# Later conversion of three weight quarters, and v pooled by additions, in a fused attention and two-MoE kernel

## The chip, the cores and the metric

The kernel runs on one core of a Trainium2 chip. The metric is the device time of one launch in microseconds, the median of several runs. A profile of one further execution shows what every engine did: TensorE (PE, matmuls; its weight loads are PEld), VectorE (DVE), ScalarE (ACT), GpSimd (POOL), and SyncE (SP), whose queue issues all the transfers of this kernel.

## The reference

Three layers follow each other. 8 sequences of 576 tokens give 4608 tokens, the model has 512 columns and 8 heads of 64.

```python
def _attn_ref(q, k, v):
    ...
    k_p = k.reshape(B, H, Sp, pool, D).mean(axis=3)      # 576 rows -> 72
    v_p = v.reshape(B, H, Sp, pool, D).mean(axis=3)
    scores = scale * np.matmul(q, k_p.transpose(0, 1, 3, 2))
    ...                                                  # softmax
    return np.matmul(attn, v_p).astype(np.float32)

def _moe_ref(x, w_in, w_out):
    h = x @ w_in                                         # 512 -> 2048
    r = np.maximum(h, 0.0)
    g = r * r
    return (g @ w_out).astype(np.float32)                # 2048 -> 512

def _moe2_ref(x, phi, w1, w2):                           # soft MoE: 8 experts, 32 slots
    logits = x @ phi
    ...
    return (c @ slot_out).astype(np.float32)
```

The weights `w_in` and `w_out` arrive as 64-bit floats.

## The kernel before, in words

The 4608 tokens are 36 tiles of 128. For each tile the attention's result x (4 blocks of 128 columns) goes into the first layer. That layer is the bulk of the work: for a tile t and a quarter j of w_in's 2048 columns, a **unit** (t, j), it does 12 matmuls of 128x512 (L453) into one PSUM buffer named `l1`, in two halves of 6. There are two such buffers. ACT takes a relu of the result (L466, into `r`), and DVE (L473) or ACT (L475) multiplies, which gives `g`. A third unit can only start when the `g` (where DVE made it, it reads the PSUM buffer itself) of the first is done. Each `g` is stored to DRAM (L477).

The order of everything else is a table: `at(slot, fn)` hangs a step behind the half unit with that number, 288 slots in all. `paced` holds a step until the last relu before it, `pinned(name, ...)` until a marked instruction, `behind_l1` until the last matmul of the first layer. The scheduler then sets each engine's order, and every engine works through its own queue in order: an instruction that waits holds all that stand behind it.

Two kinds of side work lie in the first 250 us, and the change touches both.

**Weights.** A quarter of a 64-bit weight matrix is loaded as four pieces of 512 KB (`load_w`, L373) into one of two staging buffers, `st0` and `st1`, which take turns over the eight loads (four of w_in, four of w_out). Each piece is one chunk and is turned into 32-bit numbers by six instructions (`f32_steps`): ACT L342, then DVE L344, L347 and L351, then an addition L355 and the last DVE step L356. For w_out all of the last five are on DVE, and the result overwrites the staging buffer. Chunk c of w_out's quarter j stands at slot s0 + 3c with s0 = 26 + 12j. At s0 + 13 the quarter is stored (L413), at s0 + 14 to s0 + 17 PE transposes it (L418) and ACT copies it out (L420, `wt`), at s0 + 22 a product with phi follows (L426, copied by DVE L428 to `at_sb`), at s0 + 25 another (L434).

**Pooling.** k and v of one sequence come in four pieces of two heads (72 rows x 1024 numbers, L150) into a ring of three `kv` buffers. Groups of 8 tokens are added up. For sequences 0, 1 and 2 (`PEP`) PE does it for k, and `pool_v_dve` for v: one DVE reduction (L189) that reads the 1024 numbers with a stride. For sequence 3 and later, `pool_kv` does three additions on POOL for each piece, of 512, 256 and 128 columns (L157, L158, L159).

Of the kernel before, what the change touches and what calls it, by code (L numbers as in the profile page):

```python
# [11 lines left out]
U32 = mybir.dt.uint32  # L12
# [5 lines left out]
def kernel(  # L18
# [12 lines left out]
    nc = tc.nc  # L31
# [8 lines left out]
    P = 128  # L40
# [22 lines left out]
    stp = ctx.enter_context(tc.tile_pool(name="stp", bufs=1))  # L63
# [10 lines left out]
    vpp = (kvp, a3)  # L74
# [24 lines left out]
    q_t, raw_k, raw_v, kp_t, vp_t = {}, {}, {}, {}, {}  # L99
# [259 lines left out]
        )  # L359
        yield dst  # L360

    st_t, mark, n_st = {}, {}, [0]
    eng = {"P": nc.gpsimd, "V": nc.vector}
    w_in64 = w_in.bitcast(U32).rearrange("(k p) (f two) -> p k f two", p=P, two=2)
    w_out64 = w_out.bitcast(U32).rearrange("(c p) (d two) -> p c d two", p=P, two=2)

    def load_w(kind, j, i0=0, i1=4):
        if i0 == 0:
            st_t[kind, j] = stp.tile([P, 4, 512, 2], U32, tag=f"st{n_st[0] % 2}", name="st")
            n_st[0] += 1  # L370
        src = w_in64[:, :, j * QF:(j + 1) * QF] if kind == "in" else w_out64[:, j * CPQ:(j + 1) * CPQ]
        for i in range(i0, i1):
            nc.sync.dma_start(out=st_t[kind, j][:, i], in_=src[:, i])  # L373
# [393 lines left out]
    def at(slot, fn, *a):  # L767
        ev.setdefault(slot, []).append((fn, a))
# [64 lines left out]
    for t in range(6, NT):  # L833
# [3 lines left out]
    units = [  # L837
        (0, 0), (0, 1), (1, 0), (3, 1), (3, 0), (1, 1), (2, 0), (0, 2),
        (2, 1), (2, 2), (1, 2), (3, 2), (0, 3), (2, 3), (3, 3), (1, 3),
    ]  # L840
    units += [(t + u, j) for t in range(NI, NT, 2) for j in range(NQ) for u in range(2)]

    for j in range(PC, NQ):
        for kk in range(KD):
            at(CS[j - 2][kk], paced, conv_in, j, kk)
    at(0, load_w, "in", 2)
    at(3, load_w, "in", 3)
    for j in range(NQ):
        s0 = 26 + 12 * j
        at((17, 31, s0 - 8, s0 - 8)[j], load_w, "out", j)  # L850
        for c in range(CPQ):
            at(s0 + 3 * c, paced, conv_out, j, c)
        at(s0 + 13, store_wo, j)
        for kk in range(KD):
            at(s0 + 14 + kk, behind_l1, turn_wo, j, kk)
        at(s0 + 22, behind_l1, fold_phi, j)
        at(s0 + 25, behind_l1, sum_a, j)
# [11 lines left out]
    for t in (NT - 4, NT - 2):  # L869
        s0 = SLOTS * t  # L870
# [13 lines left out]
    for t in range(0, ND, 2):  # L884
        s0 = 96 + 28 * (t // 2)
# [5 lines left out]
    for b in range(1, B):  # L891
        s0 = a_at[b * S // P]
        for i in range(NPAIR):
            at(s0 - 16 + 2 * i, load_kv, k, raw_k, b, i)
            if b in PEP:
                at(s0 - 12 + 2 * i, pool_k, b, i)
            else:
                at(s0 - 12 + 2 * i, pool_kv, nc.gpsimd, raw_k, kp_t, b, i, kvp, "kp")
            at(s0 - 10 + 2 * i, load_kv, v, raw_v, b, i)
            if b in PEP:  # L900
                at(s0 - 4 + 2 * b - 2 + 2 * i, pool_v_dve, b, i, vpp[b % 2])
            else:
                at(s0 - 4 + 2 * i, pool_kv, nc.gpsimd, raw_v, vp_t, b, i, vpp[b % 2], "vp")
        if b not in PEP:
            at(s0 - 4, make_kb, b)
# [271 lines left out]
```

## Time and profile before

| | |
|---|---|
| median of 3 runs | 774.43 us (772.29 to 775.55) |
| the profiled execution | 766.02 us |
| its span, first to last instruction | 764.2 us |
| PE busy | 723.5 us (95%) |
| DVE busy | 532.0 us (70%) |
| ACT busy | 392.1 us (51%) |
| POOL busy | 132.1 us (17%) |
| mean granted clock of TensorE | 0.980 of full speed |

The profiled execution was 8.4 us shorter than the median of the runs. An engine's busy time is the sum over its instructions; the share is that of the span. Whether an engine's wait matters is not seen from the share but from the chain of waits: who released whom, and what PE stood idle for.

### The profile page before, as it was taken

Reading aid. Unit: us, or ns where it says so; the run is one execution under the profiler, and the core shown is the slowest. Engines: PE = TensorE matmul, PEld = TensorE weight load, DVE = VectorE, ACT = ScalarE, POOL = GpSimd, SP = SyncE. Lnnn points to the kernel's source line nnn. Section 1 sums busy time; section 2 is a strip of 40 time slices with the busy share of each in tenths; the row PEclk is TensorE's granted clock in tenths of the full one; section 3 lists DMA queues with packets and bytes.
Section 4 is the critical chain, followed back from the end, with each engine's and each line's share of the span. In section 5 each row is a group of like instructions: output and inputs, shape, how many; then the busy total and the mean of one; then the engine's idle time right before and its main releaser. Section 6 shows DMA issues by size and latency. Waiting matters only on the chain.

```text
span 764.2 us, 14453 instructions
## 1 busy us (share of the span) xinstructions
PE 723.5 (95%) x5260; PEld 511.4 (67%) x5260; DVE 532.0 (70%) x1049; ACT 392.1 (51%) x1135; POOL 132.1 (17%) x151
## 2 busy tenths in 40 slices
PE   8789999989899999999999999999999999998992
PEld 7557788777677776676666666766666676663462
DVE  4996766596936689789979787878787746324153
ACT  3685677455547464545656562737575454341142
POOL 2231300052714400050342221320000000000000
PEclk9699999999999999999999999999999999999997
DMA  8956754858655996696997788878686436979998
GB/s 276 310 181 204 232 134 135 247 146 250 166 166 151 281 250 183 185 275 177 256 285 224 194 243 241 227 216 240 177 271 199 116 96 233 415 250 352 372 313 294
DMA packets 224135, 175.10 MB, mean 229 GB/s; under 512 B 75072, under 2 KB 186688, under 8 KB 224064
## 3 DMA queue, kind: packets, MB, share of 16 engines
q1 hardware_dynamic: 224064, 174.17, 75.2%
q8 instruction: 42, 0.69, 0.4%
q14 instruction: 29, 0.24, 0.1%
HBM read 126.94 MB, written 47.19 MB: 228 GB/s over the span
## 4 chain that ended last, share of the span: by engine, by line
PE 71%; DVE 12%; DMA 7%; ACT 6%; issue 2%; SPq 0%; POOL 0%; ACTq 0%; DVEq 0%
PE l L453 44%; PE misc L633 3%; PE pl L541 3%; PE misc L1098 2%; PE gT L311 2%; ACT es L245 2%; PE att L311 2%; PE l L1066 2%; PE gT L234 2%; PE att L234 2%; PE att L541 2%; DMA kv<-in_v_dram 1%; ACT aT L284 1%; DMA st<-in_moe_w_in_dram 1%; DMA out_dram<-o 1%
## 5 line engine op out<-in xcount | busy, mean ns | idle before, releaser
L453 PE MATMUL l<-w,xh 128*128 128x512 f32 x1152 | 383.4, 412 | 10.1 <-DVE g L473 5.0
L453 PEld LDWEIGHTS l<-w,xh 128*128 128x128 f32 x1152 | 209.8, 190 | 77.1 <-issue 17.1
L453 PE MATMUL l<-w,xl 128*128 128x512 f32 x576 | 231.7, 403 | 0.0
L466 ACT ACTIVATE r<-l 128x512 f32<-128x512 f32 x144 | 86.6, 604 | 163.6 <-PE l L453 151.1
L453 PEld LDWEIGHTS l<-w,xl 128*128 128x128 f32 x576 | 109.3, 190 | 28.7 <-issue 3.9
L157 POOL TENSOR_TENSOR kv<-kv 72x512 f32<-72x512 f32 x40 | 54.0, 1356 | 211.6 <-DMA kv<-in_v_dram 112.8
L284 ACT COPY aT<-turned 32x256 f32<-32x256 f32 (+1 forms) x168 | 67.8, 404 | 21.2 <-DVE turned L293 19.2
L473 DVE TENSOR_TENSOR g<-l,r 128x512 f32<-128x512 f32 x57 | 39.0, 683 | 28.0 <-ACT r L466 21.8
L245 ACT ACTIVATE es<-att,mx 128x72 f32<-128x72 f32 x120 | 36.9, 334 | 25.3 <-DVE mx L241 25.0
L516 DVE STREAM_TRANSPOSE turned<-turned 128x1024 f32<-128x1024 f32 x39 | 47.6, 1230 | 2.5 <-DMA turned<-g_dram 1.9
L245 ACT ACTIVATE es<-gT,mx 128x72 f32<-128x72 f32 x120 | 36.8, 331 | 16.0 <-DVE mx L241 15.9
L286 DVE COPY aT<-turned 32x256 f32<-32x256 f32 (+1 forms) x120 | 38.4, 320 | 1.6
L475 ACT ACTIVATE g<-r 128x512 f32<-128x512 f32 x54 | 34.5, 640 | 0.8
L396 POOL TENSOR_TENSOR w<-tmp,w 128x512 fp32r<-128x512 f32 x16 | 22.8, 1430 | 66.6 <-ACT w L395 66.6
L158 POOL TENSOR_TENSOR kv<-kv 72x256 f32<-72x256 f32 x40 | 33.1, 833 | 0.8
L473 DVE TENSOR_TENSOR tmp<-l,r 128x512 f32<-128x512 f32 x33 | 22.5, 682 | 15.4 <-ACT r L466 12.1
L268 DVE TENSOR_TENSOR es<-es,rs 128x576 f32<-128x576 f32 x36 | 32.3, 902 | 0.7
L344 DVE TENSOR_SCALAR tmp<-tmp 128x512 uint32<-128x512 uint32 x32 | 16.3, 511 | 23.3 <-ACT tmp L342 23.3
L516 DVE STREAM_TRANSPOSE tmp<-tmp 128x1024 f32<-128x1024 f32 x25 | 30.3, 1223 | 2.9 <-DMA tmp<-g_dram 2.9
L342 ACT ACTIVATE tmp<-st 128x512 f32<-128x512 f32 x32 | 21.7, 680 | 14.5 <-DMA st<-in_moe_w_in_dram 10.3
L245 ACT ACTIVATION_READ_ACCUMULATOR es<-att,mx 128x1 f32 x120 | 26.3, 219 | 0.0
L245 ACT ACTIVATION_READ_ACCUMULATOR es<-gT,mx 128x1 f32 x120 | 26.0, 217 | 0.0
(200 smaller groups left out, 1064.1 us busy)
## 6 DMA issues: line engine op xcount, KB each, us to landing
g_dram<-g SPq DMA_DIRECT2D x95, 256.0 KB
turned<-g_dram SPq DMA_DIRECT2D x39, 512.0 KB
w<-in_moe_w_dram SPq DMA_DIRECT2D x32, 512.0 KB
tmp<-g_dram SPq DMA_DIRECT2D x25, 512.0 KB
w<-in_moe_w_dram SPq DMA_DIRECT2D x6, 2048.0 KB
g_back<-g_dram SPq DMA_DIRECT2D x40, 256.0 KB
kv<-in_k_dram SPq DMA_DIRECT2D x32, 288.0 KB
kv<-in_v_dram SPq DMA_DIRECT2D x32, 288.0 KB
```

Source lines behind the costliest of these rows:

```text
L157: eng.tensor_tensor(out=x[:, :, 0:4], in0=x[:, :, 0:4], in1=x[:, :, 4:8], op=ALU.add)
L158: eng.tensor_tensor(out=x[:, :, 0:2], in0=x[:, :, 0:2], in1=x[:, :, 2:4], op=ALU.add)
L245: mark["es", t] = nc.scalar.activation(out=es[:, e], in_=sv[:, h], func=AF.Exp, bias=mx[:, e:e + 1], accum_out=rsum[:, t % 8, e, 0:1],)
L268: mark["norm", t] = nc.vector.tensor_tensor(out=es, in0=es, in1=rs.unsqueeze(2).to_broadcast([P, H, SP]), op=ALU.mult)
L284: nc.scalar.copy(out=dst, in_=src)
L286: eng[e].tensor_copy(dst, src)
L453: mm = mark["l1", t, j] = nc.tensor.matmul(hp_t[t, j], steps[i][0], steps[i][1], start=(i == 0), stop=(i == 2 * n - 1))
L466: nc.scalar.activation(out=r, in_=hp, func=AF.Relu, scale=1.0 / (R * R if sq == "V" else R))
L473: mark["sq"] = nc.vector.tensor_tensor(out=dst, in0=pre, in1=src, op=ALU.mult)
L475: nc.scalar.activation(out=dst, in_=src, func=AF.Square)
L516: nc.vector.transpose(out=gc.rearrange("p (n i) -> p n i", i=32), in_=gc.rearrange("p (n f) -> p n f", f=32))
L541: mark["logits"] = nc.tensor.matmul(pl[32 * c:32 * c + 32], a_sb[:, c, 32 * j:32 * j + 32], gT[:, c], start=(alone or j == 0), stop=(alone ...
```

## The change

For the last three quarters of w_out the whole group of steps moves to later slots: s0 goes from 26, 38, 50, 62 to 26, 40, 54, 70, so by 0, 2, 4 and 8 half units. The loads go from slots 17, 31, 42, 54 to 20, 28, 45, 59. The staging buffer no longer alternates by a counter: quarter j of w_in uses `st0` for even j, quarter j of w_out uses `st1` for even j. w_out's quarter 0 so follows w_in's quarter 3 and its quarter 1 follows w_in's quarter 2, which is free sooner. For v of the sequences 1 and 2, the reduction L189 is replaced by the three additions of `pool_kv`, on DVE; those of sequence 2 are held until the latest `g` that DVE makes, those of sequence 1 until a matmul of the first unit.

```diff
-    st_t, mark, n_st = {}, {}, [0]
+    st_t, mark = {}, {}
...
         if i0 == 0:
-            st_t[kind, j] = stp.tile([P, 4, 512, 2], U32, tag=f"st{n_st[0] % 2}", name="st")
-            n_st[0] += 1
+            st_t[kind, j] = stp.tile([P, 4, 512, 2], U32, tag=f"st{(j + (kind == 'out')) % 2}", name="st")
...
     for j in range(NQ):
-        s0 = 26 + 12 * j
-        at((17, 31, s0 - 8, s0 - 8)[j], load_w, "out", j)
+        s0 = (26, 40, 54, 70)[j]
+        at((20, 28, 45, 59)[j], load_w, "out", j)
...
             if b in PEP:
-                at(s0 - 4 + 2 * b - 2 + 2 * i, pool_v_dve, b, i, vpp[b % 2])
+                at(
+                    s0 - 4 + 2 * b - 2 + 2 * i, pinned, ("l1", units[0][0], 0) if b == 1 else "sq",
+                    pool_kv, nc.vector, raw_v, vp_t, b, i, vpp[b % 2], "vp",
+                )
             else:
                 at(s0 - 4 + 2 * i, pool_kv, nc.gpsimd, raw_v, vp_t, b, i, vpp[b % 2], "vp")
```

The lines L342 to L477 of the kernel before stand one line earlier in the changed one from L373 on (L473 is L472 there).

The first place is DVE around the `g` of unit (6, 0), the first unit of tile 6, where v of sequence 2 is pooled. `vp_1635` (`vp_1643` in the changed kernel) is the pooled v, `st_1133` and `st_1076` are the staging buffer of w_out's quarter 1, `l1_1587` and `l1_1589` the result of unit (6, 0). The kernel before, in DVE's order:

```order
L189 TENSOR_REDUCE vp_1635<-kv_1495 72x128
L351 SCALAR_TENSOR_TENSOR tmp_124<-st_1133,tmp_124 128x512
L189 TENSOR_REDUCE vp_1635<-kv_1540 72x128
L428 COPY at_sb_1599<-misc_1594 128x4x4x32
L355 TENSOR_TENSOR tmp_124<-tmp_124 128x512
L189 TENSOR_REDUCE vp_1635<-kv_1585 72x128
L473 TENSOR_TENSOR g_1613<-l1_1587,r_1614 128x512
```

The changed kernel at the same `g`:

```order
L171 TENSOR_SCALAR kb0_119<-att_1544 64x72
L427 COPY at_sb_1601<-misc_1596 128x4x4x32
L472 TENSOR_TENSOR g_1615<-l1_1589,r_1616 128x512
L157 TENSOR_TENSOR kv_1424<-kv_1424 72x2x256
L344 TENSOR_SCALAR tmp_124<-tmp_124 128x512
L347 TENSOR_SCALAR tmp_124<-tmp_124 128x512
L158 TENSOR_TENSOR kv_1424<-kv_1424 72x2x128
L351 SCALAR_TENSOR_TENSOR tmp_124<-st_1076,tmp_124 128x512
L159 TENSOR_TENSOR vp_1643<-kv_1424 72x128
L472 TENSOR_TENSOR g_1681<-l1_1647,r_1682 128x512
```

All pooling of sequence 2's v moved from ahead of this `g` to behind it; its first piece now stands, with part of a conversion, ahead of the next `g` of DVE, that of unit (7, 0).

The second place is DVE at the conversions of w_out's quarter 2 (`st_1783`) in the kernel before, around the `g` of units (8, 0) and (9, 0):

```order
L473 TENSOR_TENSOR g_1971<-l1_1951,r_1972 128x512
L344 TENSOR_SCALAR tmp_124<-tmp_124 128x512
L347 TENSOR_SCALAR tmp_124<-tmp_124 128x512
L351 SCALAR_TENSOR_TENSOR tmp_124<-st_1783,tmp_124 128x512
...
L241 TENSOR_REDUCE mx_1989<-gT_1998 128x4
L344 TENSOR_SCALAR tmp_124<-tmp_124 128x512
L347 TENSOR_SCALAR tmp_124<-tmp_124 128x512
L351 SCALAR_TENSOR_TENSOR tmp_124<-st_1783,tmp_124 128x512
L473 TENSOR_TENSOR g_2063<-l1_2006,r_2064 128x512
```

In the changed kernel DVE comes from the `g` of unit (8, 0) to that of (9, 0), `g_2045`, and of (8, 1), `g_2103`, with attention's steps alone, and then meets two conversions of quarter 3 (`st_1893`) ahead of the `g` of unit (8, 2), `g_2204`:

```order
L472 TENSOR_TENSOR g_2045<-l1_1995,r_2046 128x512
...
L472 TENSOR_TENSOR g_2103<-l1_2053,r_2104 128x512
L344 TENSOR_SCALAR tmp_124<-tmp_124 128x512
L347 TENSOR_SCALAR tmp_124<-tmp_124 128x512
L351 SCALAR_TENSOR_TENSOR tmp_124<-st_1893,tmp_124 128x512
L355 TENSOR_TENSOR tmp_124<-tmp_124 128x512
L356 SCALAR_TENSOR_TENSOR st_1893<-tmp_124 128x512
L344 TENSOR_SCALAR tmp_124<-tmp_124 128x512
L347 TENSOR_SCALAR tmp_124<-tmp_124 128x512
L351 SCALAR_TENSOR_TENSOR tmp_124<-st_1893,tmp_124 128x512
L472 TENSOR_TENSOR g_2204<-l1_2191,r_2205 128x512
```

No conversion stands between the `g` of (8, 0) and of (9, 0) any more; two stand ahead of that of (8, 2), three units after (9, 0).

The third place is SP's queue, where the first two loads of w_out are issued. Before, `st_858` is quarter 0 and `st_1133` quarter 1:

```order
L373 DMA st_858<-in_moe_w_out_dram 128x1024 x4
...
L150 DMA kv_1255<-in_k_dram 72x2x512
L150 DMA kv_1310<-in_k_dram 72x2x512
L150 DMA kv_1382<-in_k_dram 72x2x512
L477 DMA g_dram2_104<-g_898 128x4x128
L373 DMA st_1133<-in_moe_w_out_dram 128x1024 x4
```

After, `st_1076` is quarter 1 and `st_905` quarter 0:

```order
L372 DMA st_1076<-in_moe_w_out_dram 128x1024 x4
...
L150 DMA kv_1263<-in_k_dram 72x2x512
L372 DMA st_905<-in_moe_w_out_dram 128x1024 x2
L476 DMA g_dram2_104<-g_893 128x4x128
L372 DMA st_905<-in_moe_w_out_dram 128x1024 x2
L150 DMA kv_1318<-in_k_dram 72x2x512
L476 DMA g_dram2_104<-g_938 128x4x128
L150 DMA kv_1384<-in_k_dram 72x2x512
```

The two loads changed places: the quarter that is converted first is now loaded second, at the place where quarter 1 stood, and ahead of two loads of k instead of behind them.

## Rows read from the trace of the kernel before

**Rows 1.** The page: busy time of the engines, and the chain that ended last.

```profile
PE 723.5 (95%) x5260; PEld 511.4 (67%) x5260; DVE 532.0 (70%) x1049; ACT 392.1 (51%) x1135; POOL 132.1 (17%) x151
...
PE 71%; DVE 12%; DMA 7%; ACT 6%; issue 2%; SPq 0%; POOL 0%; ACTq 0%; DVEq 0%
```

**Rows 2.** What PE waited for, 126 to 232 us: total, times, longest.

```profile
PE l L453 <- DVE g L473: 4.3, 2, 2.7
PE gT L299 <- ACT wt L420: 1.0, 1, 1.0
```

**Rows 3.** PE's timeline: start, duration, [idle before <- releaser].

```profile
196.06 0.60 PE L418 MATMUL gT<-ident,st 128*128 128x128 f32 x4
199.34 0.73 PE L453 MATMUL l<-w,xh 128*128 128x512 f32 x2 [2.67 <-DVE g L473]
...
210.76 0.66 PE L311 MATMUL gT<-aT,vp 72*64 72x128 f32 x8
```

**Rows 4.** L453 in three stretches: length, PE busy, PEld busy, granted clock, DMA.

```profile
147.29:150.09 2.80, 2.80 (x14) 2.24 (x12) 1.00 0.70 217
156.30:159.29 2.99, 2.99 (x9) 2.34 (x7) 0.50 1.07 374
200.99:203.13 2.14, 2.14 (x7) 1.65 (x5) 0.50 0.91 158
```

**Rows 5.** 20 us of all engines: PE, PEld, DVE, ACT, POOL busy, clock, DMA.

```profile
140.00:160.00 20.00, 18.40 (x124) 14.18 (x121) 14.50 (x22) 7.87 (x27) 6.48 (x5) 0.91 0.80 261
```

**Rows 6.** DVE's timeline around the `g` of unit (6, 0).

```profile
146.83 2.01 DVE L189 TENSOR_REDUCE vp<-kv 72x128 f32<-72x1024 f32 x1 [2.03 <-DMA kv<-in_v_dram]
...
152.46 1.91 DVE L189 TENSOR_REDUCE vp<-kv 72x128 f32<-72x1024 f32 x1
154.28 0.69 DVE L473 TENSOR_TENSOR g<-l,r 128x512 f32<-128x512 f32 x1
```

**Rows 7.** The chain that ended last, in order of time: two transfers of v.

```profile
133.77 3.88 DMA kv<-in_v_dram
139.67 7.13 DMA kv<-in_v_dram
```

**Rows 8.** DVE's timeline ahead of the third stall.

```profile
190.17 1.50 DVE L347 TENSOR_SCALAR tmp<-tmp 128x512 uint32<-128x512 uint32 x1
191.71 1.10 DVE L351 SCALAR_TENSOR_TENSOR tmp<-st,tmp 128x512 f32<-128x512 uint32 x1
...
198.60 0.69 DVE L473 TENSOR_TENSOR g<-l,r 128x512 f32<-128x512 f32 x1
```

**Rows 9.** ACT's timeline there: the relu of the same unit.

```profile
195.60 0.63 ACT L466 ACTIVATE r<-l 128x512 f32<-128x512 f32 x1
```

**Rows 10.** POOL's timeline: first additions of sequence 3.

```profile
152.24 1.42 POOL L157 TENSOR_TENSOR kv<-kv 72x512 f32<-72x512 f32 x1 [59.25 <-PE gT L234]
...
188.67 2.71 POOL L157 TENSOR_TENSOR kv<-kv 72x512 f32<-72x512 f32 x2 [7.54 <-DMA kv<-in_k_dram]
```

**Rows 11.** DVE operations by line: count, ns min/median/max, first and last start.

```profile
L347 DVE TENSOR_SCALAR tmp<-tmp x32: 409/420/1504, 11.0 to 206.2; 128x512 uint32<-128x512 uint32 x32
L351 DVE SCALAR_TENSOR_TENSOR tmp<-st,tmp x32: 674/692/1646, 11.5 to 207.2; 128x512 f32<-128x512 uint32 x32
L189 DVE TENSOR_REDUCE vp<-kv x10: 1905/1980/2030, 17.3 to 152.5; 72x128 f32<-72x1024 f32 x10
L355 DVE TENSOR_TENSOR tmp<-tmp x32: 670/688/1342, 12.2 to 208.0; 128x512 f32<-128x512 f32 x32
L556 DVE TENSOR_TENSOR plsb<-plsb,att x21: 277/603/648, 286.3 to 682.8; 128x256 f32<-128x256 f32 x15, 128x128 f32<-128x128 f32 x6
```

**Rows 12.** SP's timeline: the second load of w_out.

```profile
88.14 1.80 SPq L373 DMA_DIRECT2D st<-in_moe_w_out_dram  x4
```

**Rows 13.** ACT's timeline: the first chunk of w_out, and the relu after it.

```profile
94.65 0.71 ACT L342 ACTIVATE tmp<-st 128x512 f32<-128x512 f32 x1
...
96.63 0.60 ACT L466 ACTIVATE r<-l 128x512 f32<-128x512 f32 x1 [0.75 <-PE l L453]
```

## The prediction

> **What bounds the kernel now.** I read the busy times first: PE works 95% of the span and owns 71% of the chain that ended last, DVE 12% [rows 1]. So the kernel is a PE stream with a few holes. A step on another engine counts only where PE stands still for it, and since PE is the bound to the end, a hole that is closed in the middle shortens the whole. The second view is what PE waited for, in the stretch where conversion of w_out and pooling of v meet, 126 to 232 us. It names three holes, two on a `g` made by DVE, 4.3 us together, and one of 1.0 us on ACT's copy of a transposed w_out [rows 2]. The larger of the two is 2.67 us at 199.34 [rows 3], so the other is 1.6 us and the sum of all three 5.3 us.
>
> The third view is the granted clock around them. Twelve matmuls L453 took 2.80 us at clock 1.00 (0.233 us each), but seven took 2.99 us behind the first hole and five took 2.14 us behind the third, both at 0.50 [rows 4]: 0.43 us each, the lower of the two levels (1.2 instead of 2.4 GHz). These rows alone lose 7 x 0.19 = 1.4 and 5 x 0.19 = 1.0 us. The slow stretch is a little longer than them: the mean clock over 140 to 160 us is 0.91 [rows 5], and 0.09 x 20 = 1.8 us is then the most that it lost there. I take 1.5 us behind each of the two large holes, none behind the small one. What the three holes cost is so 5.3 + 2 x 1.5 = 8.3 us.
>
> Who is late in each? **First hole:** the `g` of unit (6, 0) starts on DVE at 154.28, straight behind an L189. Ahead of it DVE idled 2.03 us on a transfer of v and then did three reductions of 2 us among other work [rows 6]. That transfer is on the chain of the kernel, 7.13 us from issue to landing, and the one ahead of it 3.88 us [rows 7]; a piece of v can only be loaded when a `kv` buffer was read out. **Third hole:** the relu of unit (9, 0) starts at 195.60 [rows 9], its `g` at 198.60 [rows 8], PE at 199.34. Two conversions stand between, as the order shows, and DVE came to them late: L347 at 190.17 took 1.50 us, L351 at 191.71 1.10 us [rows 8], against medians of 0.42 and 0.69 [rows 11], while POOL did two additions from 188.67 to 191.38 and more after it [rows 10]. **Second hole:** the same kind in small; ACT's copy was behind softmax steps that waited for DVE.
>
> **The change, part by part.** *Additions for v.* A reduction takes 1.98 us. Its three additions: 512 columns 0.69 us, 128 columns 0.28 us, and 256 columns, which lies between these two [rows 11], say 0.4: 1.4 us. Eight pieces save 8 x 0.6 = 4.6 us of DVE (bounds 2.6 and 5.8 us, if the middle one costs as much as the first or as the last). On PE's path that is worth nothing by itself: DVE is busy 70% of the span, and the work lies beside PE's units. It counts through the place: the pieces of sequence 2 now stand behind the `g` of unit (6, 0), which waits for no v any more. That closes hole one: +1.6 +1.5 = 3.1 us. What is queued behind the additions instead is the `g` of unit (7, 0), behind one piece (1.4 us) and three conversion steps (0.42 + 0.42 + 0.69 us), 2.9 us together; PE has at least a unit of 2.80 us between, so it is covered within 0.1 us as long as the v is there. The last piece of v can be loaded when the first was added, some 3.3 us after the `g` of (6, 0) (the `g`'s 0.69 us, the additions and conversion steps above with their ends), and is needed by DVE about three units and some attention, 10 us, after it. With the landing times of 3.88 and 7.13 us it comes 3 us early or 0.4 us late.
>
> *Later slots.* The conversions no longer stand ahead of the `g` of unit (9, 0): hole three, 2.7 + 1.5 = 4.2 us, goes, and with the DVE work ahead of it spread out, hole two's 1.0 us. They now stand ahead of the `g` of unit (8, 2). The chain there is the same one that the third hole shows: from relu to PE's start 199.34 - 195.60 = 3.74 us undisturbed. PE's cover there is a unit (2.80 us), two groups of transposes L418 (0.60 us each) and eight matmuls L311 (0.66 us) [rows 3]: 4.66 us. So undisturbed nothing is lost. But POOL's pooling of sequence 3 now begins later too, because its loads stand behind others in SP's queue, and can meet these conversions as it does at 190 us: + (1.50 - 0.42) + (1.10 - 0.69) = 1.5 us, a chain of 5.2 us and a hole of 0.6 us. Bounds: 0, and 2.1 us if the clock falls behind it. I take the 2.1 us, since by the orders POOL's pieces and these conversions fall into the same few units.
>
> A rule speaks against the additions too. L189, with one SBUF input, took 1.91 us at 152.46 beside POOL's addition from 152.24 on [rows 6, 10]: not slowed. The Trainium skill (SBUF — State Buffer, section SBUF: two separate sides) says that DVE and GpSimd share a port pair as an exclusive lock, which a DVE operation with two SBUF inputs takes against a GpSimd operation that reads SBUF, the other blocking fully. The slow L351 agrees with it, and by it each of the 24 additions that meets POOL would wait as L351 did. By the row the sum stays as it is; by the rule it stays too unless a `g` stands behind such an addition, and then loses 0.4 us for each. In SP's order the first load for POOL stands behind those of sequence 2's v, so few can meet; I put no term on it.
>
> *Staging buffers.* The swap frees w_out's second buffer earlier. Nothing on PE's path waited for that. What it costs is the load of quarter 0, now second in SP's queue: about at 88.14 us [rows 12] instead of first. Its first chunk is due on ACT at 94.65 [rows 13], 6.5 us later. With a landing of 3.88 us it is there; with 7.13 us [rows 7] it is 0.6 us late. ACT had 0.75 us to spare before its next relu at 96.63 [rows 13], which hides that. I take 0.
>
> Stores, transposes and products of w_out keep their number and move with the slots, into stretches in which PE is full anyway.
>
> **The sum.** 8.3 - 2.1 = 6.2 us. Against the profiled 766.02 us that gives 759.8 us; against the median of 774.43, which is 8.4 us above that execution, 768.2 us. I take the difference as the same in both.
>
> **The rivals.** *(a) The wait for v only moves.* If the last piece of v lands later than 10 us, DVE stands in front of its addition with a `g` behind it, as at 146.83. Against it: 3 us to spare in the faster of the two landings; for it: none in the slower. It takes back a hole like the first, 3.1 us: gain 3.1 us, 771.3 us. The same size comes out if a new hole of 1.6 us opens at any one other place behind the moved conversions. *(b) Quarter 0 lands late.* A landing of 9.7 us rather than 7.1 us would hold ACT 3.2 us, less 0.75 us of spare: a hole of 2.4 us and 1.5 us of clock, 3.9 us back, gain 2.3 us, 772.1 us. Against it: no landing in the rows is that long. *(c) Slower: POOL on the conversions.* Quarters 2 and 3 are converted 4 and 8 half units later, and POOL's pooling moves as well. Each time that POOL's additions lie on a conversion with a `g` behind it, a hole like the third opens, 4.2 us. One more than the one that I count leaves a gain of 2.0 us (772.4 us), two more cost 2.2 us (776.6 us), three 6.4 us (780.8 us). It decides the sign from two on. For it: eight pieces of sequence 3 on POOL and eight conversions fall, by the orders, into the same stretch of some 40 us. Against it: in the kernel before they do so too, and only one large hole came of it. *(d) The change closes no hole*, since what makes `g` late is something else (ACT, or the transfers as such): no difference, 774.4 us. Against it: order and trace name the same instructions ahead of both `g`.
>
> **How the numbers follow.** Forecast 0.50, (a) 0.15, (b) 0.05, (c) 0.22 (one hole more 0.06, two 0.06, three or more 0.10), (d) 0.08. The forecast's own range is 766.1 us (no new hole, all 8.3 us) to 770.5 us. What a measurement of this kernel can tell from no change is about 0.5%, 3.9 us. Faster by more than that: 0.48 of the forecast, 0.05 of (a) and (b) if their hole is smaller than priced, 0.53. Slower by more: three holes of (c) and a part of two, 0.12. The rest, 0.35, is the same. For 8 in 10 the range runs from 765.0 us, a little below the case without a new hole for the 0.5 us that the slow stretches may have cost more, to 776.6 us, the two-hole case of (c).
>
> **What would show it.** Right: in the changed kernel PE has no hole in front of the unit that waits for the `g` of (6, 0), nor for that of (9, 0); the mean clock of the stretches at 150 and 200 us is 1.00; additions on DVE of about 0.69, 0.4 and 0.28 us; first conversion of w_out without an idle ACT ahead of it. Wrong: a wait of DVE for v in front of L157 with a `g` behind it (a); an L342 that waits for the load (b); L347 of over 1 us beside POOL's L157 between 190 and 230 us, with a PE hole on the next `g` (c); holes one and three unchanged (d). My number fails above all if the hole that I put at unit (8, 2) is not there (2.1 us lower) or is not the only one.

## The result, and the profile after

The changed kernel takes 764.06 us (median of 6 runs, 760.21 to 767.24), the kernel before on the same chip 772.69 us (6 runs, 769.76 to 775.55): a ratio of 0.9884, 95% interval 0.9853 to 0.9916, faster by 9.0 us of 772.69 (6.5 to 11.4). The forecast was 768.2 us, from 765.0 to 776.6: the sign was right, the gain half as large again as the 6.2 us forecast, and the time lies 0.9 us below the range.

The profiled execution of the changed kernel is the shortest of its six, 760.21 us. Its page, against [rows 1]: span, busy times, the chain that ended last.

```profile
span 758.4 us, 14481 instructions
...
PE 718.1 (95%) x5260; PEld 508.1 (67%) x5260; DVE 532.6 (70%) x1065; ACT 391.0 (52%) x1135; POOL 131.3 (17%) x151
...
PE 64%; DVE 16%; DMA 9%; ACT 5%; issue 2%; SPq 2%; POOL 1%; DVEq 0%; ACTq 0%; POOLq 0%
```

DVE is as busy as before, and yet the kernel is shorter: the gain is not work saved. What PE waited for from 120 to 300 us, against [rows 2] (total, times, longest):

```profile
PE l L452 <- DVE g L472: 0.4, 1, 0.4
```

The three holes of 5.3 us became one of 0.4 us, at 232 us. The windows of 20 us show it (PE, PEld, DVE, ACT and POOL busy, granted clock, DMA), the first against [rows 5]:

```profile
140.00:160.00 20.00, 20.00 (x168) 15.96 (x168) 11.98 (x28) 10.45 (x32) 0.00 (x0) 1.00 0.78 235
...
180.00:200.00 20.00, 20.00 (x110) 16.09 (x109) 14.94 (x25) 11.02 (x43) 15.87 (x17) 1.00 0.95 303
200.00:220.00 20.00, 20.00 (x126) 15.15 (x125) 18.12 (x26) 9.24 (x17) 15.55 (x16) 1.00 0.61 163
```

PE is full and its clock at 1.00. POOL's pooling of sequence 3 starts at 178.54 us instead of 152.24, later, as forecast, and lies in DVE's stretch of conversions: from 200 to 220 us DVE is busy 18.12 of 20 us.

DVE's timeline, first around the `g` of unit (6, 0) (against [rows 6]), then at that of (8, 2), then in the worst meeting with POOL, ahead of the `g` of (8, 3):

```profile
151.67 0.69 DVE L472 TENSOR_TENSOR g<-l,r 128x512 f32<-128x512 f32 x1 [1.87 <-ACT r L465]
152.28 0.68 DVE L157 TENSOR_TENSOR kv<-kv 72x512 f32<-72x512 f32 x1
...
202.77 0.61 DVE L344 TENSOR_SCALAR tmp<-tmp 128x512 uint32<-128x512 uint32 x1 [1.64 <-ACT tmp L342]
203.31 0.68 DVE L347 TENSOR_SCALAR tmp<-tmp 128x512 uint32<-128x512 uint32 x1
204.02 0.69 DVE L351 SCALAR_TENSOR_TENSOR tmp<-st,tmp 128x512 f32<-128x512 uint32 x1
204.63 0.68 DVE L472 TENSOR_TENSOR g<-l,r 128x512 f32<-128x512 f32 x1
...
208.09 1.53 DVE L347 TENSOR_SCALAR tmp<-tmp 128x512 uint32<-128x512 uint32 x1
209.66 1.67 DVE L351 SCALAR_TENSOR_TENSOR tmp<-st,tmp 128x512 f32<-128x512 uint32 x1
...
214.14 0.68 DVE L472 TENSOR_TENSOR g<-l,r 128x512 f32<-128x512 f32 x1
```

The first `g` now waits for its relu alone, not for v. At (8, 2) L347 took 0.68 and L351 0.69 us: nearly undisturbed. From 208 us on they took 1.53 and 1.67 us, worse than in [rows 8], but more stands between them and the next `g`, and PE had no hole. It was near one: 0.74 us after the start of that `g`, at 214.88, PE could have begun, and it was at other work until 215.34. PE's start behind the `g` of (8, 2), and its relu on ACT:

```profile
206.17 0.73 PE L452 MATMUL l<-w,xh 128*128 128x512 f32 x2
```

```profile
201.59 0.60 ACT L465 ACTIVATE r<-l 128x512 f32<-128x512 f32 x1 [1.75 <-PE l L452]
```

From relu to `g` it is 204.63 - 201.59 = 3.04 us, as it was at the third hole (198.60 - 195.60 = 3.00 [rows 8, 9]). At the third hole PE took 0.74 us from the start of the `g` to its own start, so here it could have begun at 205.37 us; it was at other work until 206.17. The cover, what PE had to do from the start of the relu on, was 4.58 us (forecast 4.66), the chain from there to PE's earliest start 3.78: 0.8 us to spare.

The additions, by line (count, ns min/median/max):

```profile
L157 DVE TENSOR_TENSOR kv<-kv x8: 675/678/1521, 63.2 to 161.5; 72x512 f32<-72x512 f32 x8
L158 DVE TENSOR_TENSOR kv<-kv x8: 408/410/1508, 64.0 to 163.9; 72x256 f32<-72x256 f32 x8
L159 DVE TENSOR_TENSOR vp<-kv x8: 271/276/286, 64.4 to 165.0; 72x128 f32<-72x128 f32 x8
```

By their medians 0.68 + 0.41 + 0.28 = 1.37 us a piece (forecast 1.4) against 1.98. Two of the 24 took 1.5 us, L158 at 81.78 and L157 at 88.67 us, both while POOL converted a quarter of w_in; PE had no hole there.

### The profile page after: what moved, and what is told of

It is laid out like the page before. It is cut to its first block, busy times and chain, and to the rows that moved or that the text cites. A ratio compares the mean times of both kernels' runs of the same rounds, so it can differ in the third digit from the quotient of the medians.

```text
span 758.4 us, 14481 instructions
## 1 busy us (share of the span) xinstructions
PE 718.1 (95%) x5260; PEld 508.1 (67%) x5260; DVE 532.6 (70%) x1065; ACT 391.0 (52%) x1135; POOL 131.3 (17%) x151
## 4 chain that ended last, share of the span: by engine, by line
PE 64%; DVE 16%; DMA 9%; ACT 5%; issue 2%; SPq 2%; POOL 1%; DVEq 0%; ACTq 0%; POOLq 0%
PE l L452 40%; PE misc L632 3%; PE pl L540 3%; PE misc L1100 2%; ACT es L245 2%; PE gT L311 2%; PE l L1068 2%; PE att L311 2%; DMA kv<-in_k_dram 2%; DMA st<-in_moe_w_in_dram 2%; PE gT L234 2%; DVE aT L286 2%; PE att L540 1%; DMA out_dram<-o 1%; PE att L164 1%
## 5 line engine op out<-in xcount | busy, mean ns | idle before, releaser
L157 POOL TENSOR_TENSOR kv<-kv 72x512 f32<-72x512 f32 x40 | 54.1, 1357 | 224.7 <-DMA kv<-in_v_dram 115.9
L472 DVE TENSOR_TENSOR g<-l,r 128x512 f32<-128x512 f32 x57 | 38.8, 680 | 23.3 <-ACT r L465 15.1
L286 DVE COPY aT<-turned 32x256 f32<-32x256 f32 (+1 forms) x120 | 42.8, 356 | 1.7
L472 DVE TENSOR_TENSOR tmp<-l,r 128x512 f32<-128x512 f32 x33 | 22.5, 682 | 16.3 <-ACT r L465 14.1
L158 POOL TENSOR_TENSOR kv<-kv 72x256 f32<-72x256 f32 x40 | 32.7, 824 | 0.9
L344 DVE TENSOR_SCALAR tmp<-tmp 128x512 uint32<-128x512 uint32 x32 | 16.6, 517 | 21.5 <-ACT tmp L342 21.3
L342 ACT ACTIVATE tmp<-st 128x512 f32<-128x512 f32 x32 | 21.5, 676 | 17.6 <-DMA st<-in_moe_w_in_dram 13.3
L268 DVE TENSOR_TENSOR es<-es,rs 128x576 f32<-128x576 f32 x36 | 29.6, 824 | 0.8
```

The costliest lines, as they stand in the source:

```text
L157: eng.tensor_tensor(out=x[:, :, 0:4], in0=x[:, :, 0:4], in1=x[:, :, 4:8], op=ALU.add)
L158: eng.tensor_tensor(out=x[:, :, 0:2], in0=x[:, :, 0:2], in1=x[:, :, 2:4], op=ALU.add)
L286: eng[e].tensor_copy(dst, src)
L472: mark["sq"] = nc.vector.tensor_tensor(out=dst, in0=pre, in1=src, op=ALU.mult)
```

## The experiments

All ratios are against the kernel before in the same session, with 95% intervals. "Hole" is idle time of PE. A profile is one execution and need not lie near the median of its runs (that of the additions alone took 770.43 us, their median is 766.98), so the length of a hole is not to be set against a ratio to the microsecond. `...` in a cut of code stands for changed lines that are shown elsewhere.

**One part alone.** The additions with their hold on the old slots and buffers:

```diff
-                at(s0 - 4 + 2 * b - 2 + 2 * i, pool_v_dve, b, i, vpp[b % 2])
+                at(
+                    s0 - 4 + 2 * b - 2 + 2 * i, pinned, ("l1", units[0][0], 0) if b == 1 else "sq",
+                    pool_kv, nc.vector, raw_v, vp_t, b, i, vpp[b % 2], "vp",
+                )
```

> The kernel before with the additions for v alone (held behind the latest g, old slots, alternating staging buffers). Theory (three separate holes, each closed by what stands ahead of one g): the hole at the g of unit (6, 0) and its slow clock go, 3.1 us; the one at unit (9, 1) stays at about 2.7 us with a clock of 0.50 behind it; about 769.6 us against 772.7, ratio 0.996. Rival (the additions are worth their shorter DVE time, which brings all later g forward): both holes go, ratio 0.989 as in the full change. Second rival (only the slots matter): ratio 1.000, hole of 1.6 us still there.

Measured 0.9937 (0.9910 to 0.9964), 4.9 us. PE's timeline:

```profile
201.50 0.73 PE L453 MATMUL l<-w,xh 128*128 128x512 f32 x2 [3.18 <-DVE g L473]
```

The first hole is gone, the third stayed, at 3.18 us. The theory holds on the holes, both rivals fall; but the clock, which it expected at 0.50 behind that hole, stayed at 1.00. The second hole, on ACT's `wt`, is gone too.

The slots and buffers with the old reductions:

```diff
-        s0 = 26 + 12 * j
-        at((17, 31, s0 - 8, s0 - 8)[j], load_w, "out", j)
+        s0 = (26, 40, 54, 70)[j]
+        at((20, 28, 45, 59)[j], load_w, "out", j)
...
```

> The changed slots and staging buffers, with the reductions for v where they were. Theory: the hole at unit (9, 1) goes with its clock, 4.2 us, and the 1.0 us hole at L299; the one ahead of unit (6, 0)'s successor stays, 1.6 us and slow clock, since three reductions stand ahead of that g; ratio 0.993. Rival (all comes from the additions): ratio 1.000, 2.7 us hole still there. Rival (the first hole too was due to the conversions in it): no hole, ratio 0.989.

Measured 0.9926 (0.9898 to 0.9954), 5.7 us. The second and the third hole are gone, the first grew, which the expectation had not foreseen. DVE's timeline, PE's, and the chain that ended last:

```profile
154.75 3.65 DVE L189 TENSOR_REDUCE vp<-kv 72x128 f32<-72x1024 f32 x2 [5.79 <-DMA kv<-in_v_dram]
158.33 0.68 DVE L472 TENSOR_TENSOR g<-l,r 128x512 f32<-128x512 f32 x1
```

```profile
159.06 1.22 PE L452 MATMUL l<-w,xh 128*128 128x512 f32 x2 [4.61 <-DVE g L472]
```

```profile
144.13 10.60 DMA kv<-in_v_dram
```

DVE stood 5.79 us on v's transfer with the `g` behind the reductions. The transfer took 10.60 us, against 7.13 in [rows 7]. Together the parts give 10.6 us by their middle values, the whole 9.0: the sum within the intervals.

**Place or price of the additions.** One reduction a piece at the place of the additions:

```diff
-                    pool_kv, nc.vector, raw_v, vp_t, b, i, vpp[b % 2], "vp",
+                    pool_v_dve, b, i, vpp[b % 2],
```

> The changed kernel, but each piece of v is reduced by one instruction, held at the same places as the additions. Theory (the place counts, not the 0.6 us that a piece's additions save): holes at the g of (6, 0) and (9, 0) stay closed, at most 0.7 us at the g of (7, 0) or (6, 2), which each have 0.6 to 1.2 us more ahead of them; ratio 0.988 to 0.990. Rival (the shorter work counts): a hole of over 1 us with a clock of 0.50 behind it at (7, 0), (6, 1) or (6, 2), ratio 0.992 or more.

Measured 0.9913 (0.9882 to 0.9944). PE's timeline, and what DVE did ahead of it:

```profile
173.00 1.04 PE L299 MATMUL att<-ident,es 128*72 128x128 f32 x8 [1.67 <-DVE es L268]
```

```profile
164.17 3.85 DVE L189 TENSOR_REDUCE vp<-kv 72x128 f32<-72x1024 f32 x2
```

No hole at the three `g` in question, but one of 1.67 us at the softmax behind two reductions, a place that neither theory named. Held reductions keep most of the gain; the shorter additions seem worth some 2 us (0.9913 against 0.9884), within the intervals' width.

The additions at their slots, without the hold:

```diff
-                    s0 - 4 + 2 * b - 2 + 2 * i, pinned, ("l1", units[0][0], 0) if b == 1 else "sq",
-                    pool_kv, nc.vector, raw_v, vp_t, b, i, vpp[b % 2], "vp",
+                at(s0 - 4 + 2 * b - 2 + 2 * i, pool_kv, nc.vector, raw_v, vp_t, b, i, vpp[b % 2], "vp")
```

> The changed kernel without the hold: the additions for v stand at their slots, so that three pieces of sequence 2 and a part of the fourth come ahead of the g of unit (6, 0) again. Theory (that g waits for v's transfers, which the hold puts out of its way): DVE idles on a transfer of v ahead of L157 or L159 with that g behind it, PE has a hole of 1 to 4 us at the next unit, ratio 0.991 to 0.994. Rival (the additions are short enough, 1.4 instead of 2.0 us a piece): no hole over 0.5 us there, ratio 0.988.

Measured 0.9902 (0.9866 to 0.9939). DVE's timeline and PE's:

```profile
151.91 0.69 DVE L157 TENSOR_TENSOR kv<-kv 72x512 f32<-72x512 f32 x1 [3.43 <-DMA kv<-in_v_dram]
...
155.04 1.51 DVE L158 TENSOR_TENSOR kv<-kv 72x256 f32<-72x256 f32 x1
```

```profile
158.56 0.73 PE L452 MATMUL l<-w,xh 128*128 128x512 f32 x2 [1.01 <-DVE g L472]
```

DVE stands 3.43 us on v again, but the `g` of (6, 0) behind it, at 153.57, still came in time for PE. The hole, 1.01 us, is one unit later, at the `g` of (7, 0), behind an addition that took 1.51 instead of 0.41 us beside POOL's first addition of sequence 3 (154.84 to 156.28); 1.05 and 0.64 us follow behind it. So neither is shown: v's wait is there, as the theory says, but it did not make the hole, and the ratio doesn't separate from 0.9884.

**Why v is late.** The kernel with slots and buffers alone, with one `kv` buffer more:

```diff
-tc.tile_pool(name="kvp", bufs=3)
+tc.tile_pool(name="kvp", bufs=4)
```

> The kernel with the changed slots and buffers and the reductions where they were, with four kv buffers in the ring instead of three, so that the pieces of v need not wait until one is read out. Theory (the hole at the g of (6, 0) comes from v landing late): DVE's idle time of 5.8 us on v's transfer shrinks to under 1 us, the 4.6 us hole to under 1 us, ratio 0.988 against 0.9926 with three. Rival (the reductions' own time makes that g late): a hole of 2 us or more stays.

Measured 0.9979 (0.9950 to 1.0007). DVE's timeline and PE's:

```profile
153.57 1.98 DVE L189 TENSOR_REDUCE vp<-kv 72x128 f32<-72x1024 f32 x1 [1.03 <-DMA kv<-in_v_dram]
...
161.10 0.69 DVE L472 TENSOR_TENSOR g<-l,r 128x512 f32<-128x512 f32 x1 [1.96 <-ACT r L465]
```

```profile
79.07 0.80 PE L452 MATMUL l<-w,xh 128*128 128x512 f32 x1 [2.38 <-ACT w L394]
```

The waits on v fell to 1.26 and 1.03 us, and the `g` waited for its relu alone: that hole came from v landing late. Why it landed late is not separated. With three buffers SP issued the last two pieces of v at 144.13 us and later, straight behind the four pieces of a quarter of w_out (141.46 to 144.03); with four it issued three pieces of v first and that load behind them (150.94). So the ring or the load ahead of v may be the reason. The expected 0.988 was missed, since the fourth buffer moved the order elsewhere: holes of 2.38 and 1.00 us opened at 79 us, and the granted clock was 0.77 from 80 to 100 us, 4.6 us lost. Together that is 8.0 us, about what the ratio is too high by (0.0099, 7.7 us). The time does not speak on the hole; the trace does.

**POOL beside the conversions.** The additions alone, and POOL leaves out the two larger of its three additions for each piece of sequence 3, so that 2 of 8 rows are pooled:

```diff
+        if b != 3:
             eng.tensor_tensor(out=x[:, :, 0:4], in0=x[:, :, 0:4], in1=x[:, :, 4:8], op=ALU.add)
             eng.tensor_tensor(out=x[:, :, 0:2], in0=x[:, :, 0:2], in1=x[:, :, 2:4], op=ALU.add)
...
```

> The kernel with the additions alone (old slots), in which POOL leaves out the two larger additions of each piece of sequence 3, so that k and v of that sequence are pooled from 2 of 8 rows; this removes some 17 us of POOL's work from 188 us on. Theory (POOL's additions slow the conversions ahead of the g of unit (9, 0)): L347 and L351 there go back to 0.42 and 0.69 us, the hole shrinks from 3.2 us to under 1 us, ratio 0.988 to 0.990 against 0.9937 with POOL at work. Rival (the two conversions and ACT's L342 make that g late by themselves): the hole stays over 2 us, ratio as with POOL at work.

Measured 0.9870 (0.9828 to 0.9912), against 0.9937 with POOL at work. DVE's timeline and PE's (lines one later, L348 is L347):

```profile
195.30 0.42 DVE L348 TENSOR_SCALAR tmp<-tmp 128x512 uint32<-128x512 uint32 x1
195.76 0.69 DVE L352 SCALAR_TENSOR_TENSOR tmp<-st,tmp 128x512 f32<-128x512 uint32 x1
196.37 0.68 DVE L474 TENSOR_TENSOR g<-l,r 128x512 f32<-128x512 f32 x1
```

```profile
197.10 0.73 PE L454 MATMUL l<-w,xh 128*128 128x512 f32 x2 [0.69 <-DVE g L474]
```

The conversions are back at their medians and the hole shrank from 3.18 to 0.69 us: POOL made the third hole large. The same edit in the changed kernel:

> The changed kernel, in which POOL leaves out the two larger additions of each piece of sequence 3 (pooled from 2 of 8 rows), so that little of POOL's work lies beside the conversions. Theory (in the changed kernel POOL still slows conversions, but PE has cover at each g, so that this costs nothing): L347 and L351 after 190 us back near 0.42 and 0.69 us, and yet the ratio stays at 0.988, within 0.003. Rival (the 0.6 us hole and slow clock that I priced at unit (8, 2), or others of that kind, are paid somewhere): ratio 0.984 or less.

Measured 0.9866 (0.9818 to 0.9915), against 0.9884: no difference that can be told, and PE's only hole from 57 to 300 us was 0.2 us. In the changed kernel the meetings are covered. That rests on the traces, which have no hole with POOL's work or without it; the interval alone would leave room for a cost of some 5 us, and the rival's 0.984 lies in it.

**Which slots.** The changed kernel with the last quarter at its old slots:

```diff
-        s0 = (26, 40, 54, 70)[j]
-        at((20, 28, 45, 59)[j], load_w, "out", j)
+        s0 = (26, 40, 54, 62)[j]
+        at((20, 28, 45, 54)[j], load_w, "out", j)
```

> The changed kernel with w_out's last quarter alone back at its old slots (start 62, load 54). Theory (the hole at unit (9, 1) comes from that quarter's conversions standing around the g of units (9, 0) and (8, 1), where POOL slows them): a hole of 1 to 3 us on one of these units, L347 or L351 of over 1 us ahead of it, ratio 0.992 to 0.994. Rival (the moves by 2 and 4 half units are what matters, or the hold alone): no hole over 0.5 us, ratio 0.988.

Measured 0.9952 (0.9923 to 0.9981). PE's timeline, and DVE's ahead of it:

```profile
198.79 0.73 PE L452 MATMUL l<-w,xh 128*128 128x512 f32 x2 [2.04 <-DVE g L472]
```

```profile
193.65 2.72 DVE L356 SCALAR_TENSOR_TENSOR st<-tmp 128x512 uint32<-128x512 uint32 x2
...
196.38 1.40 DVE L347 TENSOR_SCALAR tmp<-tmp 128x512 uint32<-128x512 uint32 x1
```

The hole is back, 2.04 us, behind slowed conversions. The opposite, the held additions and the move of the last quarter alone:

```diff
-        s0 = 26 + 12 * j
-        at((17, 31, s0 - 8, s0 - 8)[j], load_w, "out", j)
+        s0 = (26, 38, 50, 70)[j]
+        at((17, 31, 42, 59)[j], load_w, "out", j)
...
```

> The kernel before with two edits alone: the held additions, and w_out's last quarter moved by 8 half units (start 70, load 59); quarters 1 and 2, and the alternating buffers, as before. Theory (these two edits close the two large holes): no hole over 1 us from 126 to 240 us, ratio 0.986 to 0.990, as the full change. Rival (the smaller moves of quarters 1 and 2 are needed too): a hole of over 1 us at a g behind the conversions of quarter 2, ratio 0.992 or more.

Measured 0.9940 (0.9905 to 0.9975): the theory falls. PE's timeline, and DVE's ahead of it:

```profile
217.76 0.73 PE L453 MATMUL l<-w,xh 128*128 128x512 f32 x2 [1.48 <-DVE g L473]
```

```profile
210.41 1.50 DVE L344 TENSOR_SCALAR tmp<-tmp 128x512 uint32<-128x512 uint32 x1
...
212.55 1.11 DVE L351 SCALAR_TENSOR_TENSOR tmp<-st,tmp 128x512 f32<-128x512 uint32 x1
213.69 1.66 DVE L355 TENSOR_TENSOR tmp<-tmp 128x512 f32<-128x512 f32 x1
```

Both old holes are closed, but a new one of 1.48 us opened at 217.76, at the `g` of (8, 3), behind conversions of the last quarter that POOL slowed. The rival's ratio came, but not its hole behind quarter 2. The holes that its profile shows from 120 to 300 us (this and one of 0.76 us) do not add up to the 4 us that the ratio is short of the full change. The two intervals overlap, though, and the profiled execution, 764.31 us, is 2.8 us below the median of its runs; whether there is a rest, and where, is open.

**The buffers.** The changed kernel with the alternating counter:

```diff
...
-            st_t[kind, j] = stp.tile([P, 4, 512, 2], U32, tag=f"st{(j + (kind == 'out')) % 2}", name="st")
+            st_t[kind, j] = stp.tile([P, 4, 512, 2], U32, tag=f"st{n_st[0] % 2}", name="st")
+            n_st[0] += 1
```

> The changed kernel with the staging buffers alternating by the counter as before. DVE's order is that of the changed kernel. Theory (the swap is worth nothing on PE's path): ratio 0.988 to the kernel before, no hole over 0.5 us from 60 to 240 us. Rival (the swap is needed for the later slots, or it costs time through quarter 0's load coming second): a wait of ACT L342 or DVE for a load of w_out, ratio differing from 0.988 by over 0.004, either way.

Measured 0.9879 (0.9848 to 0.9911) against 0.9884 with the swap, PE from 120 to 300 us without a hole over 0.3 us: no worth of the swap can be told, within intervals of some 2.5 us each way.

**The kernel before, again.** Two more profiles of it, with no edit.

> The kernel before, a second look. Theory (the size of the hole at the g of (6, 0) hangs on when v lands and so differs from run to run): that hole differs by over 1 us from the 1.6 us of the first profile. Rival (it is a fixed part of the kernel): 1.6 us within 0.3.

> The kernel before, a third look. Theory: holes on g and their neighbours between 126 and 232 us sum to 5 to 9 us, each large one of another size than in the first two profiles (1.6 and 2.7; 1.3 and 3.2), as v's landing and POOL's timing fall. Rival: the same sizes within 0.3 us as in one of them.

They took 775.28 and 769.38 us. PE's timeline in the second look, then in the third:

```profile
59.77 1.14 PE L311 MATMUL att<-aT,vp 72*64 72x128 f32 x16 [0.58 <-ACT aT L300]
...
158.81 0.73 PE L453 MATMUL l<-w,xh 128*128 128x512 f32 x2 [1.27 <-DVE g L473]
...
204.78 0.73 PE L453 MATMUL l<-w,xh 128*128 128x512 f32 x2 [3.20 <-DVE g L473]
```

```profile
56.26 1.14 PE L311 MATMUL att<-aT,vp 72*64 72x128 f32 x16 [0.58 <-ACT aT L300]
...
156.58 0.74 PE L453 MATMUL l<-w,xh 128*128 128x512 f32 x2 [1.93 <-DVE g L473]
...
200.70 0.73 PE L453 MATMUL l<-w,xh 128*128 128x512 f32 x2 [2.47 <-DVE g L473]
```

The large holes were 1.27 and 3.20 us, then 1.93 and 2.47; with the smaller ones beside them PE stood 8.0 and 6.7 us from 126 to 232 us, against 5.3 in the first profile. The first hole moved by 0.3 us each way, less than the 1 us that the second look's expectation asked for, so that theory falls; what grew there were the small ones behind it. The third look's large holes differ by 0.3 and 0.2 us from those of the first, which is the rival's "within 0.3" or just beyond it; their sum with the small ones lies in the 5 to 9 us expected. So the large holes differ little from run to run, the small ones beside them more, and the profile that the forecast rests on had the least. Its clock fell more: from 140 to 220 us the windows of 20 us lose 3.6 us by it there, and 1.8 us in each of the other two. Holes and clock together are 8.9, 9.8 and 8.5 us.

The first line of each marks a second point: the same step of the opening starts at 59.77 and 56.26 us, in the first profile of before at 55.64, and in the changed kernel's at:

```profile
57.65 1.14 PE L311 MATMUL att<-aT,vp 72*64 72x128 f32 x16 [0.57 <-ACT aT L300]
```

The program up to there is the same. What differs is the granted clock at the very start (the first 20 us of the second look):

```profile
0.00:20.00 20.00, 16.37 (x169) 15.69 (x170) 5.78 (x22) 4.40 (x8) 3.93 (x16) 0.77 0.88 251
```

In the five profiles of this case in which it was 0.74 to 0.77 there, that step starts at 59.28 to 59.77 us; in the nine in which it was 1.00, at 55.64 to 58.66. What lies behind that step is 764.2 - 55.64 = 708.6, 773.5 - 59.77 = 713.7 and 767.6 - 56.26 = 711.3 us before, and 758.4 - 57.65 = 700.8 us after: 10.5 us less than the mean of the three. It is 702.5 us in the profile with the alternating buffers, 8.7 us less, so the gain does not hang on the one short execution.

## Why the prediction was wrong in size

**Which holes, and whose.** Right. Both large holes closed, and each part closes its own, as the two single-part kernels show. For the first hole the place behind the `g` is enough, since the held reductions leave none there; that it is needed is not shown, since the additions without the hold left none at that `g` either. And the way to the third hole was told too short. The prediction has DVE come late to the two conversions. In the kernel before DVE stood idle ahead of the second one, for ACT, and ACT had stood at the softmax for DVE:

```profile
196.82 0.54 DVE L344 TENSOR_SCALAR tmp<-tmp 128x512 uint32<-128x512 uint32 x1 [0.80 <-ACT tmp L342]
```

```profile
193.21 0.32 ACT L245 ACTIVATE es<-gT,mx 128x72 f32<-128x72 f32 x1 [3.30 <-DVE mx L241]
```

L241 is DVE's next work behind the slowed L347 and L351, and the relu of (9, 0) and L342 stand behind that softmax on ACT: PE began the last matmul of (9, 0) at 192.55 us, and the relu began at 195.60. So POOL's price reached the `g` by way of ACT and its relu as well. With the additions alone that wait of ACT was 3.09 us, with POOL's work lighter 1.70. In the changed kernel no conversion stands between: the relu of (9, 0) starts at 190.35 and its `g` at 191.99, 1.64 us later instead of 3.00.

A slip in the text on the change: `st_1783` is the buffer of w_out's quarter 3, not 2. So the third hole belonged to the last quarter, the one that moved by 8 half units, which is what the experiment with that quarter at its old slots shows.

**The term that failed: the new hole at unit (8, 2), 2.1 us.** It did not come. Chain and cover were right as sums (3.78 and 4.58 us against 3.74 and 4.66 forecast). The chain agrees because it is the same row of steps in both places: relu, L342 behind it on ACT, L344, L347, L351, `g`. The cover agrees by luck: two groups of transposes took 0.35 us each from start to start, not 0.60, and sixteen L311 stood there, 1.02 us, not eight. What failed is the 1.5 us for POOL. DVE waited 1.64 us for L342 ahead of that conversion, so what POOL slowed earlier was made up in that wait, and only the steps behind it counted. Nor was that one lucky execution: five of the kernels above have the same slots (slots alone, held reductions, old buffers, no hold, four `kv` buffers), and in their profiles DVE waited 0.28 to 3.61 us there, L347 took 0.42 to 0.97 us and L351 0.69 to 0.83, and PE had no hole at that place. The prediction gave both bounds, 0 and 2.1, and took the upper. Without it the sum is 8.3 us, 766.1 us. That a hole of this kind is possible at the next `g` of DVE is shown too: the kernel with the held additions and the last quarter moved has one of 1.48 us at (8, 3), where the changed kernel had 0.46 us to spare.

**The base.** The kernel before came to 772.69 us over 6 runs, 1.7 us below the 774.43 that the sum was taken from. With 2.4 us of gain missed (8.6 us between the medians against 6.2), that makes the 4.1 us by which 768.2 is too high. The range moved with it: taken from 772.69 it would have begun at 763.3 us.

**"The difference as the same in both."** It isn't. The profiled execution lay 8.4 us below the median before, and 3.85 us below it after. So 759.8 us, the forecast against the profiled execution, came out at 760.21 by luck. The 8.3 us of the sum stand better than that: the profile that they come from had small holes (5.3 us against 8.0 and 6.7) but more of the slow clock, and with it the three profiles of before lose 8.9, 9.8 and 8.5 us.

**The parts.** The additions' own part, forecast at 3.1 us, measured 4.9 (2.8 to 6.9), and the slots', forecast at 5.2 before the deduction, 5.7 (3.6 to 7.9). The second hole, 1.0 us, which the sum gives to the slots, is gone with either part alone; counted with the additions it makes their forecast 4.1 us. The 0.4 us for an addition of 256 columns came true (0.41) as a guess: the row that it was read from has 128x256 operations too, at 0.60 us [rows 11].

**Terms at nothing.** The buffers' swap: no difference that can be told, and no hole. The 4.6 us of DVE time, forecast to be worth nothing by itself: mostly so, though held reductions cost 1.67 us at a softmax, 2 us in the ratio without being separated from 0. Covers at (7, 0): no hole, as forecast. Additions that meet POOL: none of sequence 2's did in the changed kernel. Without the hold one did, with the `g` of (7, 0) behind it, and it lost 1.1 us, not the 0.4 us that the prediction would have priced.

**The rivals.** (a) did not come: DVE had no wait on sequence 2's v. (b) did not come: ACT waited for no load of w_out. (c) half: POOL slowed about as many conversion steps as before (from 140 to 240 us 11 took over 0.35 us more than their line's median, against 9, 11 and 10 in the three profiles before), L347 up to 1.53 us, without a hole on PE; its price was right only where little stands between conversion and `g`. (d) falls.

**The clock.** Of the two falls that I counted at 1.5 us each, neither comes in the changed kernel. But they are not in every run of the kernel before, as below.

## What to carry to other kernels

Read a hole backwards along the late engine's own queue: what stands ahead of the late instruction there, and what that waited for, and follow it onto the other engine where it waited. Moving work behind it costs nothing if the next such instruction has cover; shortening it elsewhere buys little. Slow neighbours (here POOL beside DVE) count only where chain and cover are within a microsecond or two of each other, so price each place by that difference, not by the worst row. And take the sizes of holes, and what the clock loses behind them, from more than one execution.

## What the runs showed of the hardware

A fall of the granted clock did not follow from the length of the hole ahead of it. L453 behind the 3.18 us hole with the additions alone, then behind the two large holes of the third look at before, and behind the 4.61 us hole with the slots alone (length, PE busy, PEld busy, clock, DMA):

```profile
201.50:206.70 5.20, 3.06 (x12) 2.17 (x12) 1.00 0.54 104
```

```profile
156.58:161.50 4.92, 4.92 (x15) 3.86 (x16) 0.65 0.93 303
200.70:205.60 4.90, 3.06 (x12) 2.18 (x12) 1.00 0.73 154
```

```profile
159.06:164.00 4.94, 4.94 (x12) 3.92 (x13) 0.50 0.68 182
```

It stayed at 1.00, the level of 2.4 GHz, behind 3.18 and 2.47 us, and fell behind 1.93 and 4.61 us, in the last case to 0.50, the level of 1.2 GHz. So a fixed 1.5 us per hole, as I took it, is a mean at best: the six large holes in the three profiles of before lost 7.2 us by the clock together, 1.2 us each.

POOL's additions slow DVE operations with one SBUF input as well: L347, which reads one, took up to 1.53 us beside them in the changed kernel instead of 0.42, and with the additions alone 1.51 us ahead of the third hole, where it took 0.42 again without POOL's larger additions. The one reduction L189 that met POOL stayed at 1.91 us [rows 6, 10].
